# Attention's sums turned on TensorE, inverted there and stored as seven rows, with the periodic order placed anew

## The chip, the cores and the metric

One core of a Trainium2 chip runs the whole program in one launch. The metric is the device time of an execution in microseconds; the number quoted is the median over several runs.

## The reference

Attention with normalised q and k over 4 batches and 12 heads, then two feed-forward layers without a residual path, all in float32 on the inputs' values:

```python
# q, k, v: (4, 12, 448, 64)
q_n, k_n = rmsnorm(q, g_q), rmsnorm(k, g_k)
scores = matmul(q_n, k_n.T) / sqrt(64)
attn = exp(scores - max(scores, axis=-1))
attn = attn / (sum(attn, axis=-1) + 1e-9)
x = matmul(attn, v)                       # to (1792, 768)
h = x @ moe_w_in;  x = silu(h) @ moe_w_out        # 768 -> 2048 -> 768
h = x @ moe2_w_in; out = relu(h)**2 @ moe2_w_out  # 768 -> 2048 -> 768
```

## The kernel before, in words

The kernel is written as a list of steps. Each step has a kind, an engine (or a choice of engines) with an estimated duration, a function that issues its instructions, and the buffers that it reads and writes. A planner at build time orders all steps per engine. Most steps of the attention are *fixed*: the tables LOADS and TABLE give the place of a step within a period, PERIOD is the distance from one pair to the next, and FIRST adds an offset in the first eight pairs. So the nominal start of a step is PERIOD x i + table + offset, with PERIOD 9.007, and the planner keeps that order on each engine. The steps of the two layers are free: the planner simulates the engines and one DMA queue over eight rounds and keeps the best order. What is issued is only an order; on the chip every instruction starts when its engine reaches it and its semaphores allow it. SyncE (SP in the profile) issues nearly all DMAs, in its order, and stops at one whose data isn't ready.

The attention treats 24 pairs of heads, one after the other in a software pipeline. For a pair:

- `prepare` loads q and k (load_qk, two DMAs of 224 KB, L594; ring of 4), takes squares (ScalarE), sums (VectorE) and the inverse root by Newton steps (GpSimd), multiplies (norm, GpSimd), turns the result on TensorE (turn_q, L689) and splits it into an upper and a lower part (q_hi, q_lo).
- `values` loads v (load_v, 224 KB, L721; ring of 3).
- `weigh` works in four chunks of queries: 128, 128, 128 and a mixed one of the last 64 queries of both heads. A chunk has scores (TensorE, L755, or mixed, L762, which reads the masked copy Q made by GpSimd, L739), row_max (VectorE, L777), exp (ScalarE, L785), which also leaves the row sums in one of the 7 columns of `sums` (128 x 7), turn_e (TensorE, L798: 8 transposes of 64 x 112 into two banks "t" of PSUM), and e_copy (the two banks go to SBUF, one by ScalarE, one by VectorE, L559 and L561).
- `attend` multiplies with v in two halves (L851, 16 matmuls each). Beside it the sums take their own way: inverse (VectorE, L824 and L825) adds 1e-9 and takes the reciprocal in place, store_r (SyncE, L832) writes the 128 x 7 words to a DRAM tile of 7 x 128, and three spread DMAs (L840) read that back, each row repeated over 64 partitions, into R. pv_copy (ScalarE) takes the product from PSUM and attended (GpSimd, L871) multiplies it with R.
- keep_x (SyncE, L903) writes the finished 128 x 448 block of x to DRAM; x_hi and x_lo split the blocks of the first two batches for the first layer.

The layers come after it. Their buffers lie where the attention's were, so their first writes of products wait for the last attend; the first up matmuls (L1073) can run before. Weights come as 8-byte words (load_raw, L964), are turned into float32 by ScalarE and VectorE, split in two parts and kept in DRAM for later use. Both layers then run nearly without gaps on TensorE.

PSUM has three rings of banks: 4 of "s" (scores), 3 of "t" (turned tiles), 1 of "pv".

The planner counts 7 us between store_r and its landing and 5 for a spread (the table `extra` in Step).

Of the kernel before, what the change touches and what calls it, by code (L numbers as in the profile page):

```python
# [16 lines left out]
P = 128  # L17
# [6 lines left out]
PAD = 8  # L24
# [21 lines left out]
PERIOD = 9.007  # L46
# [12 lines left out]
TABLE = {  # L59
    "squares": [-13.15, -18.44],  # L60
    "sums": [-11.29, -11.24],
    "newton": [-8.75, -8.19, -8.19, -7.83, -5.41, -5.09, -4.77, -3.81, -3.49, -2.27, -1.95, -1.63, -0.09, 0.23, 0.79],
    "norm": [1.67, 2.75],
    "turn_q": [5.9, 10.18],
    "q_hi": [7.63, 11.01],
    "q_lo": [8.32, 11.64],
    "scores": [14.24, 15.38, 19.53],
    "row_max": [15.08, 17.83, 16.75, 19.89, 21.22, 22.23, 19.36],
    "exp": [16.01, 18.67, 18.06, 21.11, 22.2, 23.34, 20.5],
    "turn_e": [20.28, 20.51, 22.62, 22.98, 25.1, 25.33, 27.01],  # L70
    "e_copy": [21.72, 22.77, 23.95, 23.43, 26.04, 27.33, 28.67, 27.93],
    "mask": [14.0],
    "mixed": [18.4],
    "attend": [29.71, 34.52],
    "inverse": [30.72],
    "pv_copy": [37.19],
    "attended": [53.79],
    "x_hi": [68.41],
    "x_lo": [84.93],
}  # L80
# [30 lines left out]
class Step:  # L111
    def __init__(self, kind, on, fn, when, n):
        self.kind, self.on, self.fn, self.when, self.n = kind, on, fn, when, n
        self.needs, self.claims = {}, []
        self.at = min(on, key=lambda e: on[e][0])
        self.extra = {"store_r": 7.0, "spread": 5.0, "load_raw": 2.5, "load_raw2": 2.0, "load_y": 1.0}.get(kind, 0.0)
        self.nom = None
# [6 lines left out]
FORM = {"scores": "rows", "turn_e": "rows", "attend": "columns"}  # L124
SWITCH = 0.16
ENGINES = ("pe", "act", "dve", "pool", "sp", "none")
ROUNDS = 8
# [290 lines left out]
def kernel(  # L418
# [79 lines left out]
    def pe_t(t):  # L498
        return {"pe": (t, None, False)}
# [1245 lines left out]
```

## Time and profile before

| what | value |
|---|---|
| median of 3 runs | 1195.02 us (1189.43 to 1204.16) |
| profiled execution | 1187.26 us |
| its span, first to last instruction | 1185.4 us |
| TensorE matmul busy | 1129.0 us, 95% |
| VectorE busy | 935.1 us, 79% |
| ScalarE busy | 611.4 us, 52% |
| GpSimd busy | 293.5 us, 25% |

The profile is one execution; its time of 1187.26 us lies 1.8 us above its span, and all durations below come from it. Busy shares are means over stages: the attention fills about the first quarter of the span, the two layers the rest. PE is TensorE's matmuls, PEld its weight loads, DVE VectorE, ACT ScalarE, POOL GpSimd, SP SyncE. A matmul's end is modelled, so a busy PE may still not be at its peak.

### The profile page before, as it was taken

What the parts mean: (1) busy time and instruction counts of PE and PEld (TensorE: products, weight loads), DVE (VectorE), ACT (ScalarE), POOL (GpSimd) and SP (SyncE); (2) the same over time, 40 slices, a digit from 0 to 9 for tenths busy, and PEclk for the clock granted to TensorE, in tenths of its full rate; (3) what the DMA queues carried; (4) which work ended last, traced back from release to release, by engine and by line L of the source; (5) the groups of instructions that cost most, each with busy time, mean ns of one, the idle gap of its engine ahead of it and who ended that gap; (6) DMA issues with size and microseconds to landing.
All of it is one profiled execution on the core that took longest, in us unless ns stands there. A gap on an engine that the chain in (4) does not pass through costs nothing.

```text
span 1185.4 us, 20339 instructions
## 1 busy us (share of the span) xinstructions
PE 1129.0 (95%) x7405; PEld 1006.2 (85%) x7405; DVE 935.1 (79%) x1671; ACT 611.4 (52%) x1233; POOL 293.5 (25%) x533
## 2 busy tenths in 40 slices
PE   6997989897999999999999999999999999999998
PEld 5775766676998988999999999899999989999997
DVE  6887778674877778997678798578888986888886
ACT  5897788685455345544545352533333525333321
POOL 5666667621002010200010002001131120223220
PEclk8999999898999999999999999999999999999999
DMA  6577797758864756767878649877767695555544
GB/s 178 62 94 114 86 126 95 97 67 169 281 212 140 223 158 197 236 224 228 299 245 263 222 144 347 317 253 280 270 223 260 234 351 218 202 186 175 172 156 138
DMA packets 143988, 235.28 MB, mean 198 GB/s; under 512 B 33937, under 2 KB 107665, under 8 KB 143889
## 3 DMA queue, kind: packets, MB, share of 16 engines
q1 hardware_dynamic: 143648, 233.80, 67.4%
q8 instruction: 58, 0.95, 0.4%
q14 instruction: 42, 0.34, 0.1%
q10 hardware_dynamic: 240, 0.20, 0.1%
HBM read 157.58 MB, written 76.37 MB: 197 GB/s over the span
## 4 chain that ended last, share of the span: by engine, by line
PE 51%; DVE 8%; issue 1%; ACT 1%; DVEq 0%; ACTq 0%
PE t L1162 17%; PE s L1260 12%; PE s L1503 10%; PE pv L1162 7%; PE s L1628 5%; DVE w L580 1%; DVE g L1177 1%; DVE gg L1522 1%; DVE W L1119 0%; DVE W L1138 0%; DVE g L1560 0%; DVE gg L1680 0%; DVE gl L580 0%; DVE xf L1522 0%; DVE g L1436 0%
## 5 line engine op out<-in xcount | busy, mean ns | idle before, releaser
L1260 PE MATMUL s<-gg,w 128*128 128x448 f32 (+1 forms) x1168 | 238.6, 363 | 0.0
L1260 PEld LDWEIGHTS s<-gg,w 128*128 128x128 f32 x1168 | 217.0, 188 | 16.7
L1177 DVE TENSOR_TENSOR g<-t,g 128x448 f32<-128x448 f32 x180 | 108.7, 618 | 64.8 <-PE t L1162 58.1
L1503 PE MATMUL s<-w,gh 128*128 128x384 f32 (+1 forms) x564 | 144.0, 336 | 2.9 <-DVE gg L1522 1.8
L1522 DVE TENSOR_TENSOR gg<-s,gg 128x384 f32<-128x384 f32 (+1 forms) x197 | 102.3, 546 | 19.0 <-PE s L1503 18.9
L580 DVE TENSOR_TENSOR w<-W,w 128x768 fp32r<-128x768 f32 (+1 forms) x122 | 111.2, 918 | 3.5 <-ACT w L571 2.3
L777 DVE TENSOR_REDUCE mx<-s 128x1 f32<-128x448 f32 x168 | 100.3, 611 | 11.4 <-PE s L755 4.0
L1162 PE MATMUL t<-yb,w 128*128 128x448 f32 x468 | 103.8, 370 | 5.0 <-DVE w L580 3.3
L1503 PEld LDWEIGHTS s<-w,gh 128*128 128x128 f32 x564 | 102.1, 189 | 6.0 <-DVE gg L1522 1.9
L571 ACT CAST w<-W 128x768 fp32r<-128x768 f32 (+1 forms) x72 | 53.7, 747 | 91.9 <-DVE W L1138 23.3
L1162 PEld LDWEIGHTS t<-yb,w 128*128 128x128 f32 x468 | 88.1, 189 | 13.5 <-DVE w L580 4.4
L785 ACT ACTIVATE E<-s,mx 128x448 f32<-128x448 f32 x144 | 92.8, 650 | 12.4 <-DVE mx L777 7.9
L1428 ACT ACTIVATE g<-g 128x448 f32<-128x448 f32 x48 | 27.6, 577 | 133.8 <-DVE g L1177 133.4
L1503 PE MATMUL s<-w,gl 128*128 128x384 f32 (+1 forms) x282 | 94.6, 335 | 1.9 <-DVE gl L580 1.9
L1162 PE MATMUL pv<-xb,w 128*128 128x448 f32 (+1 forms) x330 | 72.3, 363 | 0.7 <-ACT g L559 0.7
L798 PEld LDWEIGHTS t<-ident,E 64*112 64x112 f32 x1152 | 44.5, 135 | 28.6 <-ACT PTa L559 7.4
L755 PE MATMUL s<-T 64*128 64x448 f32 x432 | 65.8, 408 | 1.1 <-ACT T L698 0.9
L1162 PEld LDWEIGHTS pv<-xb,w 128*128 128x128 f32 x330 | 60.8, 188 | 6.2 <-ACT g L559 1.3
L580 POOL TENSOR_TENSOR gl<-g,gh 128x448 fp32r<-128x448 f32 (+1 forms) x20 | 21.5, 1076 | 173.2 <-ACT gh L571 101.0
L851 PE MATMUL pv<-PTa,vv 112*64 112x256 f32 x384 | 52.0, 412 | 11.5 <-issue 6.0
L798 PE MATMUL t<-ident,E 64*112 64x64 f32 x1152 | 50.1, 225 | 12.4 <-ACT PTa L559 5.5
L1162 PE MATMUL t<-xc,w 128*128 128x448 f32 x270 | 60.0, 366 | 0.0
(179 smaller groups left out, 2356.3 us busy)
## 6 DMA issues: line engine op xcount, KB each, us to landing
raw<-in_moe_w_in_dram SPq DMA_DIRECT2D x32, 768.0 KB
raw<-in_moe_w_out_dram SPq DMA_DIRECT2D x24, 512.0 KB
raw<-in_moe_w_out_dram SPq DMA_DIRECT2D x16, 768.0 KB
su<-w SPq DMA_DIRECT2D x16, 768.0 KB
w<-su SPq DMA_DIRECT2D x16, 768.0 KB
xf<-y SPq DMA_DIRECT2D x48, 224.0 KB
xf<-x SPq DMA_DIRECT2D x39, 224.0 KB
ki<-W SPq DMA_DIRECT2D x16, 384.0 KB
```

Of the source, the lines that this page charges most:

```text
L571: nc.scalar.copy(o(), a())
L580: kind, when, any_t(n, rate), lambda e: engine(e).tensor_tensor(o(), a(), h(), ALU.subtract),
L755: nc.tensor.matmul(pts[j].ap[:, :S], T.ap[r, 0, a, c * CQ:(c + 1) * CQ], T.ap[r, 1, b_], start=(k_ == 0), stop=(k_ == 2),)
L777: lambda e, pt=pt, mx=mx: nc.vector.tensor_reduce(mx.ap, pt.ap[:, :S], AX.X, ALU.max, negate=True),
L785: lambda e, j=j, n=n, pt=pt, mx=mx, E=E: nc.scalar.activation(E.ap[:, j], pt.ap[:, :S], AF.Exp, bias=mx.ap, accum_out=sums.ap[:, n:n + 1]),
L798: nc.tensor.transpose(pe.ap[:CP, n * D:(n + 1) * D], E.ap[r, j, m * CP:(m + 1) * CP], ident.ap[r, r])
L1162: nc.tensor.matmul(pt.ap[:, c1:c2], w_()[:, c0 + c, :], view(b, a, c)()[:, c1:c2], start=(start and c == 0 and k == 0), stop=(c == HC - 1 ...
L1177: lambda e: nc.vector.tensor_tensor(o.ap, pt.ap[:, :S], a.ap, ALU.add),
L1260: nc.tensor.matmul(pt.ap[:, c1:c2], w_()[:, f, :], gg.ap[:, k, a, f, c1:c2], start=(f == 0 and n == 0), stop=(f == HQ - 1 and n == 2), ski ...
L1503: nc.tensor.matmul(pt.ap[:, :en], g.ap[:, fi, c0:c0 + P], w_()[:, 0, e0:e0 + en], start=(n == 0), stop=(n == 5),)
L1522: "acc", at, dve_t(n), lambda e: nc.vector.tensor_tensor(o(), pt.ap[:, :n], o(), ALU.add),
L1628: nc.tensor.matmul(pt.ap[:, :NH], a[i][0](m), b[j][0](), start=(start and k == 0), stop=(k == 2), skip_group_check=True,)
```

## The change

Four things change in the attention.

1. A step turn_s is added in `attend`: two transposes on TensorE (one per half of the partitions) turn the sums from 128 x 7 to 7 x 128, into columns 256 to 319 of the two banks that the pair's last turn_e uses (`pes`, returned by `weigh` as `last`).
2. inverse reads these banks: two tensor_scalar adds from PSUM into a new tile `inv` (7 x 128, ring of 2) and one reciprocal over it. The maximum that was taken along with the addition, and its buffer, go.
3. store_r writes `inv` to the DRAM tile as it lies: 7 rows of 128 words. The planner's count for its landing goes from 7 to 1 us.
4. All fixed places are new: PERIOD is 9.034, and TABLE, LOADS and FIRST have other values (FIRST, which moves the first eight pairs, isn't shown whole). Q has one buffer in place of two, and a padding tile of 8 words per partition goes.

```diff
-PERIOD = 9.007
+PERIOD = 9.034
...
-    "load_qk": [-28.41, -31.23],
-    "load_v": [16.98],
-    "store_r": [31.32],
-    "spread": [42.52, 43.02, 42.02],
-    "keep_x": [75.63],
+    "load_qk": [-27.01, -21.65],
+    "load_v": [13.9],
+    "store_r": [26.08],
+    "spread": [31.38, 30.43, 35.42],
+    "keep_x": [57.88],
...
-    "scores": [14.24, 15.38, 19.53],
+    "scores": [13.88, 14.5, 18.44],
-    "exp": [16.01, 18.67, 18.06, 21.11, 22.2, 23.34, 20.5],
-    "turn_e": [20.28, 20.51, 22.62, 22.98, 25.1, 25.33, 27.01],
-    "e_copy": [21.72, 22.77, 23.95, 23.43, 26.04, 27.33, 28.67, 27.93],
-    "mask": [14.0],
-    "mixed": [18.4],
-    "attend": [29.71, 34.52],
-    "inverse": [30.72],
-    "pv_copy": [37.19],
-    "attended": [53.79],
+    "exp": [16.11, 17.44, 18.05, 19.67, 20.78, 21.87, 22.48],
+    "turn_e": [17.85, 18.21, 20.24, 20.6, 22.28, 22.64, 24.11],
+    "e_copy": [19.19, 19.52, 21.39, 22.32, 23.09, 23.08, 25.71, 25.96],
+    "mask": [16.33],
+    "mixed": [19.62],
+    "attend": [24.96, 29.82],
+    "turn_s": [24.34],
+    "inverse": [25.31],
+    "pv_copy": [33.04],
+    "attended": [44.84],
...
-        self.extra = {"store_r": 7.0, "spread": 5.0, ...
+        self.extra = {"store_r": 1.0, "spread": 5.0, ...
...
-        Q = sa([P, 2, 2, LAST], FR, "Q", 2)
+        Q = sa([P, 2, 2, LAST], FR, "Q", 1)
...
-        def inverse(e):
-            r = sums.ap
-            nc.vector.tensor_scalar(r, r, 1e-9, None, ALU.add, ALU.max, accum_out=top.ap)
-            nc.vector.reciprocal(r, r)
+        NS = 2 * NCQ + 1
+        inv = sa([NS, P], F32, "inv", 2)
+        def turn(e):
+            for h, pe in enumerate(last):
+                r = slice(h * D, (h + 1) * D)
+                nc.tensor.transpose(pe.ap[:NS, 2 * CQ:2 * CQ + D], sums.ap[r], ident.ap[r, r])
+        step("turn_s", at, pe_t(0.06), turn, reads=[ident] + keys, writes=[(pe, "s") for pe in last])
+        def inverse(e):
+            for h, pe in enumerate(last):
+                nc.vector.tensor_scalar(
+                    inv.ap[:, h * D:(h + 1) * D], pe.ap[:NS, 2 * CQ:2 * CQ + D], 1e-9, None, ALU.add)
+            nc.vector.reciprocal(inv.ap, inv.ap)
...
-            lambda e: engine(e).dma_start(rd.ap.rearrange("n p -> p n"), sums.ap), reads=keys, writes=[rd],
+            lambda e: engine(e).dma_start(rd.ap, inv.ap), reads=[inv], writes=[rd],
```

In FIRST, pair 0's store_r has the offset 0.34 before and 0.59 after.

## Rows read from the trace of the kernel before

**Rows 1.** The page's 40 equal slices of the span, busy and clock in tenths.
```profile
PE   6997989897999999999999999999999999999998
...
PEclk8999999898999999999999999999999999999999
```

**Rows 2.** Busy time in stretches of the span; clock, DMA share and GB/s stand last.
```profile
core 0: us, PE busy (x) PEld busy (x) DVE busy (x) ACT busy (x) POOL busy (x), PEclk, DMA share, GB/s
...
30.00:277.50 247.50, 223.26 (x2687) 163.33 (x2687) 194.87 (x391) 203.55 (x532) 148.92 (x374) 0.96 0.70 96
...
33.50:45.00 11.50, 11.28 (x146) 8.14 (x142) 10.12 (x20) 9.86 (x27) 6.33 (x21) 1.00 0.40 27
...
53.40:62.60 9.20, 9.20 (x121) 6.89 (x119) 8.55 (x19) 8.69 (x24) 6.07 (x16) 1.00 0.43 74
...
83.07:216.00 132.93, 119.31 (x1434) 87.30 (x1434) 105.53 (x209) 111.31 (x293) 92.27 (x231) 0.96 0.77 105
...
216.00:276.10 60.10, 52.10 (x613) 37.69 (x613) 41.69 (x88) 43.79 (x112) 22.83 (x47) 0.91 0.60 88
...
277.00:290.00 13.00, 11.16 (x70) 9.64 (x66) 3.84 (x5) 1.90 (x3) 1.15 (x1) 1.00 0.94 128
...
5.00:11.00 6.00, 2.65 (x25) 2.41 (x23) 3.05 (x8) 2.88 (x5) 0.00 (x0) 1.00 0.99 272
```

**Rows 3.** SyncE in order of time: start us, us, DMA issued, count.
```profile
33.26 0.39 SPq L832 DMA_DIRECT2D rd<-sum  x1
...
53.53 0.38 SPq L832 DMA_DIRECT2D rd<-sum  x1
...
62.71 0.38 SPq L832 DMA_DIRECT2D rd<-sum  x1
...
72.13 0.38 SPq L832 DMA_DIRECT2D rd<-sum  x1
...
84.58 1.21 SPq L903 DMA_DIRECT2D x<-xf  x1
...
102.01 0.32 SPq L721 DMA_DIRECT2D vv<-in_v_dram  x1
...
216.00 0.39 SPq L832 DMA_DIRECT2D rd<-sum  x1
...
276.12 0.38 SPq L832 DMA_DIRECT2D rd<-sum  x1
```

**Rows 4.** TensorE in order of time, three stretches; in brackets the idle before.
```profile
52.41 1.95 PE L851 MATMUL pv<-PTa,vv 112*64 112x256 f32 x16
...
56.79 0.61 PE L798 MATMUL t<-ident,E 64*112 64x64 f32 x16
...
57.33 1.52 PE L851 MATMUL pv<-PTb,vv 112*64 112x192 f32 x16
...
61.60 1.95 PE L851 MATMUL pv<-PTa,vv 112*64 112x256 f32 x16
...
114.99 3.68 PE L851 MATMUL pv<-PTa,vv 112*64 112x256 f32 x16 [3.75 <-issue]
...
293.65 3.78 PE L1073 MATMUL t<-xc,w 128*128 128x448 f32 x10 [5.50 <-ACT g L1086]
```

**Rows 5.** Groups of VectorE instructions up to 290 us, shapes kept apart.
```profile
L561 DVE COPY PTb<-t 112x512 f32<-112x512 f32 x24 | 16.3, 679 | 0.4 <-PE t L798 0.4
...
L561 DVE COPY PTb<-t 112x256 f32<-112x256 f32 x24 | 9.9, 414 | 7.4 <-PE t L798 4.0 <-PE s L755 2.5 <-PE t L689 0.8
...
L825 DVE RECIPROCAL sum<-sum 128x7 f32<-128x7 f32 x24 | 4.8, 201 | 0.8
...
L824 DVE TENSOR_SCALAR_CACHE_REDUCE sum<-sum 128x7 f32<-128x7 f32 x24 | 3.6, 149 | 0.0
...
L824 DVE DVE_READ_ACCUMULATOR sum<-sum 128x1 f32 x24 | 2.0, 81 | 0.0
```

**Rows 6.** ScalarE in order of time around the end of the attention.
```profile
290.09 0.89 ACT L971 ACTIVATE W<-raw 128x768 f32<-128x768 f32 x1 [10.69 <-DMA raw<-in_moe_w_in_dram]
```

More of the change, by code (lines that the diff above doesn't have):

```diff
@@ new lines @@
+    1: {"load_qk": [18.88, 13.97], "squares": [13.43, 9.0], "sums": [9.44, 9.44], "load_v": [-6.03], "newton": [8.12, 7.92, 7.92, 6.9, 5.88, 4.79, 4.16, 3.07, 3.07, 3.07, 3.07, 3.07, 3.07, 3.07, 3.07], "norm": [2.97, 2.29], "turn_q": [1.0, 0.58], "q_hi": [0.54, 0.56], "q_lo": [0.58, 0.59], "scores": [0.55, 0.55, 0.55], "row_max": [0.55, 0.55, 0.55, 0.55, 0.55, 0.55, 0.55], "exp": [-0.19, -0.19, -0.19, 0.52, 0.55, 0.55, 0.55], "turn_e": [0.55, 0.55, 0.55, 0.55, 0.55, 0.55, 0.55], "e_copy": [0.01, 0.55, 0.55, 0.55, 0.55, 0.55, -0.02, 0.55], "mask": [-2.24], "mixed": [0.55], "attend": [0.55, 0.55], "turn_s": [0.55], "inverse": [0.55], "pv_copy": [0.6], "store_r": [0.55], "spread": [0.1, 0.55, 0.55], "attended": [-2.87], "keep_x": [0.57], "x_hi": [0.83], "x_lo": [0.07]},
@@ new lines @@
+    2: {"load_qk": [10.74, 5.83], "squares": [5.78, 1.35], "sums": [4.33, 4.33], "load_v": [0.05], "newton": [3.26, 3.26, 3.26, 2.24, 1.22, 0.13, 0.13, -0.96, -0.96, -0.96, -0.96, -0.96, -0.96, -0.96, -0.96], "norm": [-0.96, -0.96], "turn_q": [0.51, 0.5], "q_hi": [-0.24, 0.48], "q_lo": [0.5, 0.51], "scores": [0.51, 0.51, 0.51], "row_max": [0.51, 0.5, 0.51, 0.5, 0.51, 0.5, 0.51], "exp": [-0.07, -0.07, -0.07, 0.48, 0.5, 0.5, 0.5], "turn_e": [0.51, 0.51, 0.51, 0.51, 0.51, 0.51, 0.51], "e_copy": [-0.03, 0.51, 0.5, 0.5, 0.5, 0.51, -0.07, 0.5], "mask": [-2.39], "mixed": [0.51], "attend": [0.51, 0.51], "turn_s": [0.51], "inverse": [0.5], "pv_copy": [0.55], "store_r": [0.5], "spread": [0.05, 0.5, 0.5], "attended": [-2.92], "keep_x": [0.52], "x_hi": [0.78], "x_lo": [0.26]},
@@ new lines @@
+    4: {"load_qk": [3.61, -0.85], "squares": [0.46, 0.45], "sums": [0.41, 0.41], "load_v": [-0.04], "newton": [-0.91, -0.91, -0.91, -0.91, -0.91, -2.0, -2.0, -3.09, -3.09, -3.09, -3.09, -3.09, -3.09, -3.09, -1.15], "norm": [-1.15, -1.15], "turn_q": [0.42, 0.41], "q_hi": [-0.16, 0.39], "q_lo": [0.41, 0.42], "scores": [0.42, 0.42, 0.42], "row_max": [0.42, 0.41, 0.42, 0.41, 0.42, 0.41, 0.42], "exp": [-0.16, -0.16, -0.16, 0.39, 0.41, 0.41, 0.41], "turn_e": [0.42, 0.42, 0.42, 0.42, 0.42, 0.42, 0.42], "e_copy": [-0.12, 0.42, 0.41, 0.41, 0.41, 0.42, 0.41, 0.41], "mask": [-2.48], "mixed": [0.42], "attend": [0.42, 0.42], "turn_s": [0.42], "inverse": [0.41], "pv_copy": [0.46], "store_r": [0.41], "spread": [0.41, 0.41, 0.41], "attended": [-1.74], "keep_x": [0.43], "x_hi": [0.69], "x_lo": [0.65]},
@@ new lines @@
+    5: {"load_qk": [-1.71, -6.17], "squares": [-0.32, 0.37], "sums": [0.37, 0.37], "load_v": [0.37], "newton": [-0.95, -0.95, -0.95, -0.95, -0.95, -2.04, -2.04, -1.98, -1.98, -1.98, -1.98, -1.98, -1.98, -1.98, -1.19], "norm": [-1.19, -1.19], "turn_q": [0.38, 0.37], "q_hi": [-0.2, 0.34], "q_lo": [0.37, 0.37], "scores": [0.37, 0.38, 0.38], "row_max": [0.38, 0.37, 0.38, 0.37, 0.38, 0.37, 0.38], "exp": [0.37, 0.37, 0.37, 0.37, 0.37, 0.37, 0.37], "turn_e": [0.38, 0.38, 0.38, 0.37, 0.38, 0.38, 0.38], "e_copy": [0.37, 0.38, 0.37, 0.37, 0.37, 0.38, 0.37, 0.37], "mask": [-2.52], "mixed": [0.37], "attend": [0.38, 0.37], "turn_s": [0.38], "inverse": [0.37], "pv_copy": [0.42], "store_r": [0.37], "spread": [0.37, 0.37, 0.37], "attended": [-1.54], "keep_x": [0.39], "x_hi": [0.65], "x_lo": [0.85]},
@@ new lines @@
+    6: {"load_qk": [-0.17, -0.08], "squares": [-0.19, 0.33], "sums": [0.33, 0.33], "load_v": [0.33], "newton": [-0.99, -0.99, -0.99, -0.99, -0.99, -2.08, -2.08, -2.02, -2.02, -2.02, -2.02, -2.02, -2.02, -2.02, -1.23], "norm": [-1.23, -1.23], "turn_q": [0.33, 0.33], "q_hi": [0.33, 0.33], "q_lo": [0.33, 0.33], "scores": [0.33, 0.33, 0.33], "row_max": [0.33, 0.33, 0.33, 0.33, 0.33, 0.33, 0.33], "exp": [0.33, 0.33, 0.33, 0.33, 0.33, 0.33, 0.33], "turn_e": [0.33, 0.33, 0.33, 0.33, 0.33, 0.33, 0.33], "e_copy": [0.33, 0.33, 0.33, 0.33, 0.33, 0.33, 0.33, 0.33], "mask": [-1.47], "mixed": [0.33], "attend": [0.33, 0.33], "turn_s": [0.33], "inverse": [0.33], "pv_copy": [0.38], "store_r": [0.33], "spread": [0.33, 0.33, 0.33], "attended": [-1.34], "keep_x": [0.35], "x_hi": [0.61], "x_lo": [1.05]},
@@ new lines @@
+    7: {"load_qk": [0.28, -0.13], "squares": [-0.24, 0.28], "sums": [0.28, 0.28], "load_v": [0.28], "newton": [-1.04, -1.04, -1.04, -1.04, -1.04, -2.13, -2.13, -2.07, -2.07, -2.07, -2.07, -2.07, -2.07, -2.07, -1.28], "norm": [-1.28, -1.28], "turn_q": [0.29, 0.28], "q_hi": [0.28, 0.28], "q_lo": [0.28, 0.29], "scores": [0.29, 0.29, 0.29], "row_max": [0.29, 0.28, 0.29, 0.28, 0.29, 0.28, 0.29], "exp": [0.28, 0.28, 0.28, 0.28, 0.28, 0.28, 0.28], "turn_e": [0.29, 0.29, 0.29, 0.29, 0.29, 0.29, 0.29], "e_copy": [0.28, 0.29, 0.28, 0.28, 0.28, 0.29, 0.28, 0.28], "mask": [-1.28], "mixed": [0.29], "attend": [0.29, 0.29], "turn_s": [0.29], "inverse": [0.28], "pv_copy": [0.33], "store_r": [0.28], "spread": [0.28, 0.28, 0.28], "attended": [-1.15], "keep_x": [0.3], "x_hi": [0.56], "x_lo": [1.24]},
@@ L123 @@
 SELF = {"pe": 0.0, "act": 0.1, "dve": 0.1, "pool": 0.06, "sp": 1.9, "none": 0.0}
-FORM = {"scores": "rows", "turn_e": "rows", "attend": "columns"}
+FORM = {"scores": "rows", "turn_e": "rows", "turn_s": "rows", "attend": "columns"}
 SWITCH = 0.16
@@ L812, in weigh, with attend @@
                 plan.fix(i, "e_copy", 2 * c + h)
-        return PT, sums
-    def attend(i, vr, PT, sums):
+        return PT, sums, pes
+    def attend(i, vr, PT, sums, last):
         b, hp = pairs[i]
```

42 lines of the change are left out of this document (17 added, 25 removed).

## The prediction

> **What bounds the kernel now.** I read the page's 40 slices first. TensorE is at 9 tenths from slice 11 on (but for the last); in the ten before it, which are the attention, it falls to 6 to 8 in half of them and its clock dips [rows 1]. So I read that stage by stretches. From 30 to 277.5 us TensorE is busy 223.26 of 247.5 us at a mean granted clock of 0.96 of full speed [rows 2]: 24.2 us idle, and, if 0.96 mixes the full 2.4 GHz with its half, (1 - 0.96) / 0.5 x 247.5 = 19.8 us at 1.2 GHz, so some 10 us of work lost. Together that is 34 us in a stage that has no other work for TensorE.
>
> Next, the pace. Each of the 24 pairs of heads issues one store of its sums from SyncE, at 33.26 us for pair 0 and at 276.12 for pair 23 [rows 3]: 242.86 / 23 = 10.56 us per pair. The order written into the kernel has a period of 9.007. Yet the best stretches do nearly what the order asks: from the store at 53.53 to that at 62.71 it is 9.18 us, to the next 9.42, and in the first of these TensorE has no gap at all: the same half of attend starts at 52.41 and at 61.60, 9.19 us apart [rows 3, 4]. So 9.19 us is TensorE's own price of a pair, and 10.56 holds 1.4 us of waiting.
>
> What it waits for is a DMA. The plainest case: the load of pair 8's values is issued at 102.01 and the attend that needs them starts at 114.99, after 3.75 us of idle TensorE; its 16 matmuls, all at half clock, then take 3.68 us in place of 1.95 [rows 3, 4]. That load is 224 KB. In the burst of loads at the start the queue moves 272 GB/s at a busy share of 0.99 [rows 2], by which 224 KB take 0.84 us.
>
> What fills the queue are the stores of the sums: 128 x 7 words that are written column by column, so 896 packets of 4 bytes for 3.5 KB. In the 11.5 us behind the first store three loads (672 KB) are all that follows, and the rate is 27 GB/s at a share of 0.40 [rows 2]. At 272 GB/s the loads need 2.47 us. By time that leaves up to 11.5 - 2.5 = 9.0 us for one store; by share it leaves 0.40 x 11.5 - 2.45 = 2.15 us. The long stretch lies between: from 83.07 to 216 us, where x is also written back from 84.58 on [rows 3], a pair takes 132.93 / 12 = 11.08 us and moves 105 GB/s x 11.08 = 1.16 MB, or 4.28 us at 272 GB/s. Elapsed time leaves 6.8 us for a store, the share (0.77 x 11.08 = 8.53) leaves 4.25. I take 6. Then the queue needs 4.3 + 6 = 10.3 us per pair, more than TensorE's 9.19: the attention is bound by its DMA queue. The pace bears this out. Before x is written back pairs can run at 9.2 to 9.4, with it at 11.08, and from 216 on, where no q and k are loaded any more, at 60.12 / 6 = 10.02, with TensorE still recovering [rows 2, 3].
>
> **The change, part by part.**
>
> *The store.* 896 packets become 7 of 512 bytes. The queue's need falls by 2.15 to 9.0 us per pair, from 11.08 to between 8.9 and 2.1. At either end it is below 9.19, so the queue stops being the bound and TensorE becomes it. This term hardly depends on what a store costs.
>
> On that cost the Trainium skill's page "DMA: Bandwidth & Descriptors" (section "Anatomy of one DMA — SWDGE (gpsimd) path") speaks against the change: it calls descriptor generation small, and says that many can be emitted before the incremental cost shows, most of a DMA's fixed time being the receipt of the write. By that a store is a fixed delay, which its new form keeps. The 27 GB/s behind the first store disagree. The rule describes the other, GpSimd path, and I give it its own rival below.
>
> *turn_s.* Two more transposes per pair (64 x 7 in, 64 columns moved), right behind the last turn_e of the pair. 16 such matmuls take 57.33 - 56.79 = 0.54 us start to start [rows 4], so two take 0.07. As a group of their own they may cost a full matmul's length more; bounds 0.07 to 0.3, I take 0.10, by the row of the same shape. It adds a wait for the last exp's sum on TensorE, with attend queued behind it. The order puts turn_s at 24.34 and the last exp at 22.48, whose row sum is there by about 23.4, so it waits only when ScalarE is late by 0.9 us. The sums' columns sit in the last turn_e's banks, which the copies at 25.71 and 25.96 hold for longer than inverse at 25.31 anyway.
>
> *inverse.* Before: 149 + 81 + 201 = 431 ns on VectorE [rows 5]. After: two small reads of PSUM and a reciprocal of 128 elements on 7 partitions. A PSUM copy of 256 elements takes 414 ns, of 512 it takes 679, or 1.035 ns per element; for 64 that gives 414 - 192 x 1.035 = 215 ns each. The reciprocal by the same rate: 201 + 121 x 1.035 = 326 ns. Sum 756 ns, 0.33 more per pair. From below: no more than 201 for the reciprocal and 149 for each read, 499. From above: all of 201 ns scales with the elements, 201 / 7 x 128 = 3.68 us. I take 0.33, since a tensor_scalar over the same 7 elements takes 149, so that most of the 201 is fixed. VectorE is busy 8.55 us of the clean 9.20 [rows 2]; 8.88 still fits under TensorE. It costs nothing while VectorE keeps 0.3 us of room; with that cover gone it costs up to 0.33 x 23 = 7.6 us.
>
> *Pace.* 9.19 + 0.10, and 0.06 for what the clean pairs show beyond the best one: 9.35. The new period, 9.034, is 0.027 above the old one, 0.6 us in all and inside this term.
>
> *Order.* Everything is placed anew: store_r at 26.08 in place of 31.32, spread from 30.43 on in place of 42.02, attended at 44.84 for 53.79, load_v at 13.9 for 16.98. Of this the depth of a pair counts once: pair 0's store stood at 31.32 + 0.34 = 31.66 and came at 33.26, 1.6 late; now it stands at 26.08 + 0.59 = 26.67 and by the same lateness comes at 28.3. SyncE works in order: behind the spreads at 30.43 and 31.38 wait x's write, load_v and load_qk. The store has 4.35 us to land before the first spread stops SyncE; seven packets behind 0.84 us of load fit into that. load_v has 24.96 - 13.9 = 11.1 us to attend, 1.7 less than before, against a load of 0.84 us behind at most 4.3 us of other bytes. The single Q buffer costs nothing: the next mask (25.36) comes 5 us after mixed (19.62) ends.
>
> So the last store comes at 28.3 + 23 x 9.35 = 243.3 in place of 276.12: **32.8 us**.
>
> *Passage to the first layer.* TensorE runs until 288.2, idles 5.50 us until 293.65 and then sits at half clock, because a load of weights lands late: ScalarE starts on it at 290.09 after 10.69 us of waiting [rows 4, 6]. In 277 to 290 the queue carries 128 x 13 = 1.66 MB, 6.1 us at 272 GB/s, at a share of 0.94; the last two stores are in front of it. Without them the load comes some 6 us sooner. Bounds 0 (other transfers fill the room) and 8 (5.5 idle and half of some 5 us at half clock); I take **4**.
>
> *The rest.* 885 us of two layers keep their work. Their free steps are ordered anew by the planner, which I count as 0, plus or minus 6.
>
> Sum against the profiled execution: 1187.26 - 32.8 - 4 = 1150.5. The median of the runs, 1195.02, lies 7.8 above that execution, and the runs spread over 1189 to 1204. If this scatter sits in the DMA waits, it goes with them; if not, it stays. I add half, 4: **1154 us**.
>
> **The rivals.**
>
> *Part of the gain.* The stores go but loads still come late in some pairs, because SyncE's order is tighter (load_v's lead is shorter) and a spread can hold it. The nearest row is the last stretch, 10.02 per pair with no loads of q and k [rows 2, 3]: 28.3 + 23 x 10.02 = 258.8, 17.3 us saved and nothing at the passage, 1170 + 4 = 1174, within 2%. For it: that stretch. Against it: the stores were still in it, and TensorE came into it from a 4 us stall. Chance 0.11.
>
> *Nothing but the depth.* A store is a fixed delay, the packets not the cause, and the pace stays 10.56: 5 us from the depth, 1187.26 - 5 = 1182, against the median 1190. This is what the skill's rule above would make of it. For it: the share of 0.40 says that the 16 engines were not full behind the first store. Against it: the 27 GB/s in the same stretch. Chance 0.05.
>
> *Slower.* VectorE becomes the bound through the reciprocal. At 3.68 us per pair inverse is 4.1, VectorE 8.55 - 0.43 + 4.1 = 12.2, and the last store comes at 28.3 + 23 x 12.2 = 309: 33 us later than before, some 1220. It decides from an inverse above 10.56 - 8.12 = 2.4 us. For it: reciprocal is the slowest of the small rows. Against it: 52 ns over the tensor_scalar of equal size. With all else that ends slower, chance 0.04.
>
> **How the numbers follow.** Forecast 0.80, part 0.11, nothing 0.05, slower 0.04. The forecast's own range: 9.19 per pair, 8 at the passage, 6 in the layers and no 4 for the scatter give 1187.26 - 36.5 - 8 - 6 = 1137; 9.6 per pair, 0 at the passage, plus 6 and the full 7.8 give 1187.26 - 27 + 6 + 7.8 = 1174. To hold 8 in 10 with the partial case it reaches 1136 to 1180. A measurement of this kernel tells about 2% from no change; 2% below the median is 1171. Of the forecast 0.77 lies under that and of the partial case 0.05: faster 0.82, same 0.14, slower 0.04.
>
> **What would show it.** Right: stores of consecutive pairs 9.3 to 9.4 us apart from first to last; the last near 243; TensorE's idle in the attention under 8 us with the clock at 1.00; no wait of attend for values; RECIPROCAL near 0.33 us; the DMA share in the attention below 0.5. Wrong: pairs above 9.8 us apart, with VectorE or the queue named; SyncE standing at the spreads for most of a period; TensorE standing at turn_s; or the gain at 243 us given back in the layers.

## The result and the profile after

The changed kernel takes 1145.24 us (median of 4 runs, 1142.44 to 1147.44) against 1195.64 for the kernel before (4 runs, 1189.43 to 1204.16): a ratio of 0.957, with a 95% interval of 0.951 to 0.964. The profiled execution takes 1145.92 us with a span of 1144.1, 41.3 us below the profiled one of before. The forecast was 1154, in a range of 1136 to 1180.

The page's 40 slices of the changed kernel answer to [rows 1]:

```profile
PE   6999999999999999999999999999999999999998
...
PEclk6999999999999999999999999999999999999999
```

From the second slice on TensorE is at 9 tenths with its full clock up to the last slice; the holes of the attention are gone. In the first slice the clock still stands at 6 tenths.

The stretches of the attention, as in [rows 2] (columns as there: clock, DMA share and GB/s last):

```profile
33.00:254.00 221.00, 214.70 (x2723) 157.71 (x2719) 213.21 (x390) 204.19 (x534) 153.79 (x380) 1.00 0.41 115
...
72.27:178.62 106.35, 102.06 (x1313) 75.74 (x1309) 102.83 (x188) 100.30 (x265) 83.64 (x207) 1.00 0.44 121
```

TensorE is busy 214.70 of 221 us, its clock is 1.00, and the queue's share is 0.44 in the middle stretch where it was 0.77, at more GB/s than before (121 for 105). But there VectorE is now the fullest engine, by a little: 102.83 of 106.35 us, against TensorE's 102.06.

SyncE's stores answer to [rows 3]; the loads, the spreads and x's writes between them are left out, and most of the stores:

```profile
33.20 0.33 SPq L840 DMA_DIRECT2D rd<-inv  x1
...
72.27 0.28 SPq L840 DMA_DIRECT2D rd<-inv  x1
...
81.88 0.28 SPq L840 DMA_DIRECT2D rd<-inv  x1
...
91.50 0.29 SPq L840 DMA_DIRECT2D rd<-inv  x1
...
253.76 0.29 SPq L840 DMA_DIRECT2D rd<-inv  x1
```

From the first to the last it is 220.56 / 23 = 9.59 us per pair. Of the 23 distances 12 are 9.60 to 9.62, seven, early and late, are 9.81 or 9.82, one is 10.21 and the last 7.25. Between 33 and 254 us no computing engine waits for a DMA, so no pair waits for a load; what makes the seven longer was not pursued. The first store comes no earlier than before. A view of the DRAM tile gives the landing of these stores:

```profile
DMA to landing us min/median/max: 2.3/3.2/5.2
```

VectorE's groups for the inverse answer to [rows 5]:

```profile
L833 DVE RECIPROCAL inv<-inv 7x128 f32<-7x128 f32 x24 | 22.6, 941 | 0.8
...
L831 DVE TENSOR_SCALAR inv<-t 7x64 f32<-7x64 f32 x48 | 8.1, 205 | 1.3 <-ACT PTb L558 0.3
```

The reciprocal over 128 elements takes 941 ns; two reads of PSUM take 205 each. At the end of the attention, TensorE in order of time answers to the last row of [rows 4]:

```profile
253.72 1.86 PE L859 MATMUL pv<-PTb,vv 112*64 112x192 f32 x16
...
255.51 1.50 PE L1081 MATMUL t<-xb,w 128*128 128x448 f32 x7
...
264.80 2.00 PE L1081 MATMUL t<-xc,w 128*128 128x448 f32 x10
```

No row from 253.72 on, into the first layer, has idle time before it: the 5.50 us gap is gone.

So 41.3 us are gained. The last attend ends at 253.72 + 1.86 = 255.6 in place of 277.30 + 1.47 = 278.8: 23.2 us. From there to the end of the span it is 888.5 us in place of 906.6: 18.1 us, which the second experiment below splits in two.

### The profile page after: what moved, and what is told of

The parts are those of the page before. It is cut to its first block, busy times and chain, and to the rows that moved or that the text cites. A ratio compares the mean times of both kernels' runs of the same rounds, so it can differ in the third digit from the quotient of the medians.

```text
span 1144.1 us, 20545 instructions
## 1 busy us (share of the span) xinstructions
PE 1119.3 (98%) x7453; PEld 1000.1 (87%) x7453; DVE 942.8 (82%) x1651; ACT 619.4 (54%) x1251; POOL 296.2 (26%) x535
## 4 chain that ended last, share of the span: by engine, by line
PE 82%; DVE 10%; issue 3%; ACT 2%; DMA 1%; POOL 1%; SPq 0%; POOLq 0%; ACTq 0%; DVEq 0%
PE t L1170 21%; PE s L1268 20%; PE s L1511 12%; PE pv L1170 8%; PE s L1636 6%; PE pv L859 4%; PE t L797 4%; PE t L1081 3%; PE s L754 2%; PE t L688 2%; DVE mx L776 2%; DVE w L579 1%; DVE ms L613 1%; PE s L761 1%; DVE PTb L560 1%
## 5 line engine op out<-in xcount | busy, mean ns | idle before, releaser
L579 DVE TENSOR_TENSOR w<-W,w 128x768 fp32r<-128x768 f32 (+1 forms) x125 | 115.2, 931 | 6.5 <-ACT w L570 5.2
L570 ACT CAST w<-W 128x768 fp32r<-128x768 f32 (+1 forms) x78 | 58.1, 746 | 90.2 <-PE s L1268 24.9
L776 DVE TENSOR_REDUCE mx<-s 128x1 f32<-128x448 f32 x168 | 96.6, 608 | 0.6 <-PE s L754 0.5
L579 POOL TENSOR_TENSOR gl<-g,gh 128x448 fp32r<-128x448 f32 (+1 forms) x22 | 25.0, 1137 | 160.4 <-ACT gh L570 91.2
L754 PE MATMUL s<-T 64*128 64x448 f32 x432 | 59.5, 397 | 0.9 <-ACT T L697 0.9
L984 ACT ACTIVATE raw<-raw 128x768 int32<-128x768 uint16 (+1 forms) x72 | 59.4, 825 | 0.0
L797 PE MATMUL t<-ident,E 64*112 64x64 f32 x1152 | 57.2, 229 | 1.8 <-ACT E L784 0.6
```

Source lines behind the costliest of these rows:

```text
L579: kind, when, any_t(n, rate), lambda e: engine(e).tensor_tensor(o(), a(), h(), ALU.subtract),
L754: nc.tensor.matmul(pts[j].ap[:, :S], T.ap[r, 0, a, c * CQ:(c + 1) * CQ], T.ap[r, 1, b_], start=(k_ == 0), stop=(k_ == 2),)
L776: lambda e, pt=pt, mx=mx: nc.vector.tensor_reduce(mx.ap, pt.ap[:, :S], AX.X, ALU.max, negate=True),
L797: nc.tensor.transpose(pe.ap[:CP, n * D:(n + 1) * D], E.ap[r, j, m * CP:(m + 1) * CP], ident.ap[r, r])
L984: lambda e: nc.scalar.activation(lo(), raw.ap[:, :2 * m].bitcast(U16).rearrange("p (m t) -> p m t", t=4)[:, :, 1], AF.Copy, bias=2.0 ** -1 ...
```

## The experiments

My theory before them: the store's packets filled the DMA queue, and without them VectorE, through the reciprocal, sets the pace of 9.61. The rivals: a store is only a delay; the order placed anew made the gain; TensorE sets 9.61.

### The words stored beside the rows

The changed kernel keeps its store of rows and adds the old one behind it, into a tile that nobody reads.

```diff
+            engine(e).dma_start(rd.ap, inv.ap)
+            engine(e).dma_start(rw.ap.rearrange("n p -> p n"), sums.ap)
```

> The changed kernel, and behind each store of 7 rows a second one of the 128 x 7 words, column by column, into a DRAM tile that nobody reads. The order of all else is unchanged. If the 896 packets fill the DMA queue (my theory), loads come late again: the queue needs 4.3 + 6 = 10.3 us per pair or more in place of TensorE's or VectorE's 9.6, attend waits for its values again, and the time is 1160 to 1180. If a store of words is only a long delay for whoever waits for it (rival), nobody waits here: stores stay 9.6 us apart and the time is 1143 to 1150.

Measured: 1221.35 us (runs of 1209 to 1235; ratio to before 1.011, 1.003 to 1.019). The direction is that of the queue, and more of it than I expected. In the profiled execution, the longest of the four at 1234.72, the first 22 stores of rows lie 13.3 us apart. The stretch and the waits in it:

```profile
30.00:320.00 290.00, 234.93 (x2620) 165.12 (x2618) 207.51 (x374) 199.50 (x515) 150.68 (x378) 0.88 0.57 78
...
POOL xf L885 <- DMA R<-rd: 52.9, 12, 6.7
...
PEld t L797 <- ACT PTb L558: 25.6, 11, 5.2
...
SPq L841 <- DMA rw<-sum: 37.1, 10, 8.0
```

A pair moves 78 GB/s x 13.3 us = 1.04 MB, or 3.8 us at 272 GB/s. Elapsed time leaves up to 9.5 us for the added store, the share (0.57 x 13.3 = 7.6 us) leaves 3.8; where between them it lies, this run doesn't say. GpSimd waits for R and TensorE for copies behind it; attend, against what I expected, waits for no values in this stretch. I had expected that nobody waits for the added store itself, but SyncE does (last row): it stands for its landing in 10 pairs, 37.1 us in all, and with it stand the loads that SyncE would issue next. So this run shows that the words cost more than the whole gain, but it doesn't part a slow queue from a long landing; a stretch in the next experiment does. That the same words cost more in the new order than in the old one (1221 against 1201 on the same chip) fits its shorter leads; that was not tried by itself. The Trainium skill's page "DMA: Bandwidth & Descriptors" (section "Measured (HBM→SBUF, 128 partitions, SWDGE, issued from GpSimd)") counts about 10.5 ns for a packet, an estimate of 9.4 us for 896. That lies within these bounds, but the trace doesn't agree that the packets themselves take this long, as the next experiment shows. The rule of the Trainium skill that the prediction weighed, by which many descriptors can be emitted before they cost anything and a store is a fixed delay, is not borne out by the time of this kernel, nor by the next one's.

### The rows alone, in the old order

The kernel before with the store in its new form; the 7 x 128 tile is filled from the identity and one sum, so that it still waits for the inverse. Beside the store only this fill, 0.53 us of VectorE per pair, and the single buffer of Q are new.

```diff
+            nc.vector.tensor_scalar(rows.ap, ident.ap[:NS, :CQ], r[:NS, 0:1], None, ALU.add)
...
-            lambda e: engine(e).dma_start(rd.ap.rearrange("n p -> p n"), sums.ap), ...
+            lambda e: engine(e).dma_start(rd.ap, rows.ap), ...
```

> The kernel before, in its own order, with the store alone in the new form: after the inverse, VectorE fills a 7 x 128 tile (identity plus one sum, some 0.2 us) and store_r writes that as 7 rows; Q has one buffer to make room. The sums don't reach the output: the division of the result by them is replaced by other numbers. If the packets are the cause, stores come 9.3 to 9.5 us apart in place of 10.56, the first layer starts without its 5.5 us gap, and the time is 1187 - 26 - 9 = 1152; the layers, whose order is that of before, keep their 16 us of idle TensorE. If the layers' 8 us of gain come from the DMAs and not from the order, they show here too and it is 1144. If the order placed anew is the cause of the gain (rival), the pace stays at 10.5 and the time above 1180.

Measured: 1147.02 us (1145.40 to 1147.70; ratio 0.953, 0.948 to 0.958), as fast as the whole change. Its first and last store, the stretch behind the first store's place in [rows 2], and its last attend:

```profile
35.94 0.34 SPq L834 DMA_DIRECT2D rd<-rows  x1
...
245.06 0.30 SPq L834 DMA_DIRECT2D rd<-rows  x1
...
33.50:45.00 11.50, 11.50 (x151) 8.66 (x151) 11.03 (x25) 10.66 (x30) 7.01 (x24) 1.00 0.22 63
...
245.95 1.47 PE L853 MATMUL pv<-PTb,vv 112*64 112x192 f32 x16
```

That is 209.12 / 23 = 9.09 us per pair in the old order (9.0 to 9.8, but for the last two of 7.95 and 5.58), and the rate in the stretch rises from 27 to 63 GB/s. A closer look at what stands behind the first store shows what the words do. Three loads follow it in both kernels, issued within 2 us. First the kernel before, then the rows alone:

```profile
34.10:34.90 0.80, 0.80 (x22) 0.79 (x22) 0.32 (x2) 0.80 (x3) 0.41 (x2) 1.00 0.53 6
34.90:44.90 10.00, 9.78 (x123) 7.10 (x119) 9.09 (x18) 8.36 (x24) 5.48 (x17) 1.00 0.41 30
```

```profile
37.40:40.40 3.00, 3.00 (x42) 2.31 (x40) 3.00 (x5) 2.16 (x8) 0.61 (x3) 1.00 0.80 231
```

The words themselves are through in 0.8 us: in the trace's records of packets, all of theirs begin between 34.18 and 34.80, some 7 ns long each. Then the loads, all issued by 35.3, move at 30 GB/s for 10 us, 0.3 MB of their 0.69; behind the rows they move at 231 GB/s and 3 us are enough. (Behind the first words of the experiment above it is 38 GB/s for 9.5 us.) The share is 0.41 meanwhile. So the words don't fill the 16 DMA engines; for some 10 us they slow down what stands behind them. By what means, no run shows.

So the store's form by itself, without the new order, is worth as much as the whole change. Its last attend ends at 247.4, 8.2 us before that of the changed kernel; after it, it takes 898.4 us. Against the 906.6 of before that is 8.2 us for the passage (same order, no gap); the changed kernel's 888.5 are another 9.9. The second layer shows where, first the kernel before, then the rows alone, then the changed kernel:

```profile
740.00:980.00 240.00, 232.63 (x1230) 219.55 (x1229) 194.01 (x320) 95.30 (x168) 38.73 (x28) 0.99 0.75 275
```

```profile
700.00:940.00 240.00, 232.66 (x1231) 219.53 (x1229) 193.94 (x319) 95.39 (x167) 38.47 (x28) 0.99 0.75 276
```

```profile
700.00:940.00 240.00, 237.88 (x1269) 225.00 (x1267) 194.10 (x323) 100.45 (x178) 42.26 (x31) 1.00 0.79 284
```

In 240 us TensorE idles 7.4 us in both kernels with the old order and 2.1 in the changed one. That part of the gain comes from the planner's placing of the free steps, not from the DMAs: behind the last attend VectorE and ScalarE run the same sequence in the first two, and another one in the third, which also moves steps between engines (ScalarE has 1233, 1233 and 1251 instructions in all).

### The reciprocal left out, and taken twice

Two edits of the one line in inverse; in both the result is multiplied by the sums.

```diff
-            nc.vector.reciprocal(inv.ap, inv.ap)
```

> The changed kernel without the reciprocal (the result is multiplied by the sums, not divided). If VectorE bounds the pace of 9.59 through the 0.94 us of the reciprocal (my theory), pairs come 9.3 us apart, TensorE's 9.19 plus turn_s, and the time falls by 23 x 0.3 = 7 to 1138. If TensorE bounds it (rival: turn_s and its waits), it stays within 1143 to 1147.

```diff
             nc.vector.reciprocal(inv.ap, inv.ap)
+            nc.vector.reciprocal(inv.ap, inv.ap)
```

> The changed kernel with the reciprocal taken twice (the result is multiplied by the sums). If VectorE bounds the pace, each pair becomes longer by 0.87 us less the some 0.3 that VectorE idles now: 10.2 to 10.5 us, and the time grows by 13 to 20, to 1158 to 1166. If TensorE bounds it with VectorE in its shadow, the 0.3 us of room take a third of it and the growth stays below 8.

Measured: 1128.75 us without it (1128.59 to 1129.21; ratio 0.938, 0.933 to 0.943) and 1167.92 with two (1167.39 to 1168.25; ratio 0.970, 0.965 to 0.975). The first half of attend in two neighbouring pairs, in the kernel without the reciprocal, with one and with two:

```profile
110.97 1.95 PE L858 MATMUL pv<-PTa,vv 112*64 112x256 f32 x16
...
119.98 1.95 PE L858 MATMUL pv<-PTa,vv 112*64 112x256 f32 x16
```

```profile
109.70 1.95 PE L859 MATMUL pv<-PTa,vv 112*64 112x256 f32 x16
...
119.31 1.95 PE L859 MATMUL pv<-PTa,vv 112*64 112x256 f32 x16
```

```profile
115.93 1.95 PE L860 MATMUL pv<-PTa,vv 112*64 112x256 f32 x16
...
126.52 1.95 PE L860 MATMUL pv<-PTa,vv 112*64 112x256 f32 x16
```

A pair takes 9.01, 9.61 and 10.59 us. The second reciprocal costs its whole length of 0.94 and a little more: VectorE sets the pace. Taking the first away gains only 0.60 of the 0.94, because then TensorE takes over:

```profile
74.00:180.00 106.00, 105.99 (x1387) 78.30 (x1387) 99.96 (x189) 105.07 (x281) 88.25 (x221) 1.00 0.47 128
```

TensorE is busy 105.99 of 106 us, with ScalarE just behind it at 105.07; which of the two sets 9.01 was not tried. So TensorE's price of a pair in the new order, with turn_s in it, is at most 9.01, less than the 9.19 of the old order without; the rival that TensorE sets 9.61 has fallen. For the kernel, one VectorE instruction costs 16.5 us, of which 23 x 0.60 = 13.8 are the pace; the first store also came 3.3 us earlier in that execution (29.94).

### The inverse taken before the turn

Here r is the sums, 128 x 7; the step is placed at 23.7, ahead of turn_s, and the copy at 25.31.

```diff
+            nc.vector.tensor_scalar(r, r, 1e-9, None, ALU.add)
+            nc.vector.reciprocal(r, r)
...
             nc.tensor.transpose(pe.ap[:NS, 2 * CQ:2 * CQ + D], sums.ap[r], ident.ap[r, r])
...
-                nc.vector.tensor_scalar(inv.ap[...], pe.ap[...], 1e-9, None, ALU.add)
-            nc.vector.reciprocal(inv.ap, inv.ap)
+                nc.vector.tensor_copy(inv.ap[...], pe.ap[...])
```

> The changed kernel with the inverse taken before the turn, on 128 x 7 in place, and only copied out of PSUM behind it. VectorE is spared the reciprocal over 128 elements: 0.15 + 0.20 + 0.33 in place of 0.33 + 0.94, some 0.6 us per pair. If VectorE alone sets 9.61, pairs come 9.0 to 9.1 us apart as without the reciprocal, and the time is 1128 to 1136 (the free steps of the layers fall into another order, worth a few us either way). If TensorE now stands at turn_s for VectorE (rival), that wait of 0.5 us or more per pair keeps it at 1140 to 1147.

Measured: 1153.87 us (1153.55 to 1155.15; ratio 0.965, 0.957 to 0.972), slower than the change. Pairs come 9.0 to 9.2 us apart at both ends, as expected, but 9.8 to 10.3 in the middle; over all 9.46. Who waits for the inverse, in us and times:

```profile
  PEld t L825: 6.1, 11
  PE t L825: 4.5, 9
```

TensorE stands at turn_s for VectorE in some 10 pairs, about half a us each (its weight loads and its matmuls wait for the same thing). So the rival is right in the middle of the attention, though the last attend still ends earlier than in the changed kernel (at 250.6). The rest is lost behind it: 901.2 us in place of 888.5, by another order of the free steps, of which I had allowed "a few us".

What makes the middle pairs long is the small add ahead of the reciprocal. One in the middle, GpSimd's product with R beside it, and one near the end:

```profile
132.63 0.99 DVE L829 TENSOR_SCALAR sum<-sum 128x7 f32<-128x7 f32 x1
...
132.45 1.15 POOL L885 TENSOR_TENSOR xf<-xf,R 128x448 f32<-128x448 f32 x1
...
238.57 0.16 DVE L829 TENSOR_SCALAR sum<-sum 128x7 f32<-128x7 f32 x1
```

In the 7 pairs in which no such product runs beside it, the add takes 0.16 us. In the other 17 it ends within 0.03 us of the product's end, after 0.8 to 1.1 us in ten of them and 0.25 to 0.27 in seven. So it waits for GpSimd, and turn_s and all of VectorE stand behind it. Why it has to wait, no run shows.

### A longer warm start, alone and with the inverse first

```diff
-        for _ in range(WARM):
+        for _ in range(90):
```

> The changed kernel with 90 in place of 40 transposes on nothing at the start, so that TensorE is busy until the first turn_q and its clock doesn't fall. If the half clock until some 27 us is what makes the first store late (33.20 against 26.7 in the order), that store comes 2 to 4 us earlier and so does the end: 1141 to 1143. If the other engines' chains set the start (rival), less than 1 us changes.

> Both of the edits: the gains add up if both theories hold, 1125 to 1133; otherwise it equals the better one of the two.

Measured: 1143.75 us (1142.37 to 1144.41; ratio 0.956, 0.949 to 0.963), and 1154.67 for both edits (1152.69 to 1155.35; 0.965, 0.956 to 0.974). Alone, the stores begin and end here:

```profile
29.52 0.34 SPq L840 DMA_DIRECT2D rd<-inv  x1
...
249.96 0.29 SPq L840 DMA_DIRECT2D rd<-inv  x1
...
12.00:28.00 16.00, 11.25 (x127) 8.41 (x126) 14.67 (x26) 11.13 (x29) 13.05 (x44) 1.00 0.68 187
```

The same stretch in the changed kernel, and with both edits:

```profile
12.00:28.00 16.00, 12.21 (x79) 8.70 (x81) 13.23 (x24) 9.52 (x23) 12.81 (x42) 0.50 0.71 189
```

```profile
12.00:28.00 16.00, 13.07 (x96) 9.40 (x93) 13.52 (x24) 9.46 (x24) 12.54 (x41) 0.68 0.70 188
```

From 12 to 28 us the granted clock is 1.00, where the changed kernel has 0.50, and the first store comes 3.7 us earlier, as does the last (3.8). Some of that is the spread between executions: the changed kernel run again, further below, has its first store at 32.41 with a clock of 0.57 there. Of the 3.7 us 1.5 show in the median, whose runs overlap with those of the change. With the inverse first, the first store doesn't come earlier (31.48, against 30.49 without the longer start) and nothing is gained: there the longer start left the clock at 0.68, so it doesn't keep the clock up by itself. That the inverse first is slower holds on one chip: with the longer start in both, 1152.69 to 1155.35 against 1142.37 to 1144.41.

### The planner's count back at 7 us

```diff
-        self.extra = {"store_r": 1.0, ...
+        self.extra = {"store_r": 7.0, ...
```

> The changed kernel with the planner's count for the store's landing back at 7 us; no instruction changes, only the order of the free steps. After the last attend the changed kernel takes 888.6 us, the rows-only kernel with before's order 898.4. If the count alone makes the better order of the layers, they take some 898 us here and the time is 1150 to 1157; if it comes from the new places of the attention's steps (rival), the time stays within 1142 to 1149.

Measured: 1166.86 us (1165.82 to 1167.31; ratio 0.975, 0.968 to 0.982), and neither theory has it all. The layers behind the last attend take 888.6 us, as in the change, so the count alone does not make their better order; but the attention takes 21 us more. With the longer count the planner puts steps of the layers into the attention, and attend waits for its bank, because ScalarE works on weights before it copies the product out (TensorE's row, then ScalarE's; L979, L984 and L570 are the weights, the last row is pv_copy):

```profile
91.24 1.95 PE L859 MATMUL pv<-PTa,vv 112*64 112x256 f32 x16 [1.38 <-ACT xf L558]
...
88.30 0.67 ACT L979 ACTIVATE W<-raw 128x512 f32<-128x512 f32 x1
88.87 0.66 ACT L984 ACTIVATE raw<-raw 128x512 int32<-128x512 uint16 x1
89.42 0.82 ACT L570 CAST w<-W 128x768 fp32r<-128x768 f32 x1
...
90.67 0.52 ACT L558 COPY xf<-pv 128x448 f32<-128x448 f32 x1
```

In the changed kernel the first step of L979 comes at 218.0 us, here at 57.7. Between 51 and 124 us stores lie 11 to 19 us apart. A figure that changes no step, only where the planner puts it, is worth 21 us.

### The turn in pv's bank

The inverse stays where VectorE has it, on 128 x 7; the turn goes behind the first half of attend, into columns of its bank that the second half fills later; the longer warm start is in. The inverse is placed at 25.31, the turn at 26.77 and the copy at 27.1.

```diff
+            r = sums.ap
+            nc.vector.tensor_scalar(r, r, 1e-9, None, ALU.add)
+            nc.vector.reciprocal(r, r)
...
+            nc.tensor.transpose(pv.ap[:NS, 2 * CQ:3 * CQ], sums.ap, ident.ap)
...
+            nc.vector.tensor_copy(inv.ap, pv.ap[:NS, 2 * CQ:3 * CQ])
...
-    "store_r": [26.08], "spread": [31.38, 30.43, 35.42],
+    "store_r": [27.75], "spread": [33.0, 32.8, 35.42],
```

> The inverse on 128 x 7 in the place where VectorE now inverts, one transpose of all 128 rows behind the first half of attend into columns of its bank that the second half fills later, and one copy of 7 x 128 behind the squares' sum; the store stands 1.7 us later, the first two spreads behind load_qk; the longer warm start is in. If VectorE sets the pace and TensorE's wait at turn_s is what made the inverse-first kernel uneven, pairs come 9.0 to 9.1 us apart throughout and the last attend ends near 240. The time is then 1128 to 1135 with the layers at 888 us, and up to 13 more if the free steps fall as they did with the inverse first. If something else bounds the pace below 9.6 (rival), the last attend stays at 249 or later.

Measured: 1140.04 us (1135.72 to 1140.76; ratio 0.959, 0.952 to 0.966). Two neighbouring attends:

```profile
103.16 1.95 PE L861 MATMUL pv<-PTa,vv 112*64 112x256 f32 x16
...
112.31 0.87 PE L861 MATMUL pv<-PTa,vv 112*64 112x256 f32 x6
```

Pairs lie 9.15 us apart nearly throughout, the last attend ends at 243.4, 12.2 us before the change's, and the layers behind it take 894.9. The theory of the pace holds: with the reciprocal over 7 elements VectorE no longer sets 9.61, and the add, with no product of GpSimd beside it, takes 0.16 us in each pair. Half of the gain goes to the free steps. Whether this kernel beats the change was tried with both on one chip:

> The changed kernel once more, unaltered, beside the next one on the same chip: 1143 to 1148, with 9.6 us per pair.

> The kernel that turns the sums in pv's bank, once more: 1136 to 1141. If it is truly faster than the changed kernel, its runs lie below all of that one's runs on the same chip, by 4 to 7 us: some 10 at the end of the attention less some 6 that its free steps lose in the layers. If the two calls differed by their chips, the runs of the two overlap.

Measured: the change 1145.69 us (6 runs, 1144.04 to 1148.65; ratio to before 0.953, 0.948 to 0.958), the other 1138.95 (6 runs, 1137.58 to 1141.18; ratio 0.947, 0.943 to 0.951). Each of its runs lies below each of the change's: it is 6.7 us faster than the change and beats both kernels. The longer warm start, 1.5 us by itself, is part of that.

## Why the prediction was right, point by point

**The bound.** Right that the stores of words hold the attention back, and shown from both sides: the store in its new form alone gives 0.953, and the old store put back beside the new one takes more than the whole gain away. The picture of it, packets that fill the queue, was not right: the words are through in 0.8 us, and what stands behind them moves at 30 GB/s for 10. One of the supports was weak, too: before x is written back three of the five distances are 9.2 to 9.4 us, the other two 10.9.

**The price of a store.** I took 6 us between 2.15 and 9.0. Both bounds took the three loads as moved within the 11.5 us; at 27 GB/s only 0.31 MB was, so they are 3.5 and 10.4. The words put back give 3.8 to 9.5, and the 10 us of slow loads speak for the upper end. As the prediction says, the term hardly depended on it.

**TensorE's pace.** 9.19 + 0.10 was to be its new price; it is at most 9.01. turn_s itself is as small as taken: its two matmuls start 0.15 us ahead of what follows them. That the new order is cheaper for TensorE by some 0.3 us I had not seen in the table; which of its neighbours saves it was not tried.

**inverse.** The step that failed: 0.33 us more per pair, from 326 ns for the reciprocal, hidden under TensorE. It takes 941, so inverse is 0.41 + 0.94 = 1.35 in place of 0.43, and VectorE is the bound at 9.61. The error was the rate: I priced a reciprocal's elements as a copy's. By (941 - 201) / 121, an estimate from these two shapes, they cost 6.1 ns each and not 1.035. The prediction had both ends and chose by the row of a 7-element tensor_scalar, where the fixed part hides the rate. The rival that VectorE becomes the bound thus came true in kind; at 1.35 us it stays short of the 2.4 from which it would have made the kernel slower.

**The pace in all.** 9.35 was 0.24 too low, or 5.5 us over 23 pairs.

**The depth.** The first store was to come at 28.3 and came at 33.20: 4.9 us too early. The lateness of before, 1.6 us, was taken over as if it were a constant. It isn't: the clock of the start differs between executions. From 12 to 28 us it is 0.50 in the changed kernel; with 0.57 the same kernel's first store came at 32.41, and with the longer warm start and 1.00 at 29.52. Nor is the clock all of it: with the inverse first, 0.60 gave 30.49 and 0.68 gave 31.48.

**The passage.** 4 us; the gap closed fully and it is 8.2, the upper bound. Without words ahead of the first weights the whole wait is gone, in the old order too.

**The layers.** 0 plus or minus 6; they gave 9.9, by the planner's placing of the free steps. The spread over the experiments, 888.5 to 901.2 us for the same work, shows that my 6 was too small.

**The scatter.** I kept half of the 7.8 us between the profiled execution and the median. The changed kernel's runs lie within 5 us, with the median 0.7 below its profiled execution. It goes with the words: the rows alone, in the old order, scatter by 2.3 us, and the words put back by 26.

Together: 32.8 + 4 + 0 = 36.8 us were forecast in the profile and 23.2 + 8.2 + 9.9 = 41.3 measured. The two terms of the attention, pace and depth, promised 9.6 us too much; passage and layers gave 14.1 more than forecast, and the scatter went whole. The stores as the cause and the queue's end as the bound hold; that the rest added up to within 9 us of the median is luck.

## What to carry to other kernels

Count the packets of a DMA, not only its bytes: behind 3.5 KB in 896 words the loads on the same queue moved at 30 GB/s for 10 us, in place of 231, and what waits for them is late, with half-clock TensorE on top. A DMA's own time doesn't show this; look at the rate behind it. Where such a store goes, look at once for the engine that is next at its limit: here 0.94 us on a nearly full VectorE cost 14 us of pace, and could be moved away by inverting before the turn, where each partition has 7 elements and not 128, at a place where TensorE doesn't wait for it. In a kernel whose free steps are ordered by a planner, a change of any cost or place moves the rest by some 10 us; compare stage by stage before a total is believed.

## What the runs showed of the hardware that I had not expected

A reciprocal of 7 x 128 on VectorE takes 941 ns and of 128 x 7 takes 201, the same 896 elements; a tensor_scalar of 7 x 64 out of PSUM takes 205. A store of 7 rows of 512 bytes lands in 2.3 to 5.2 us (median 3.2). Behind a store of 896 words of 4 bytes, itself through in 0.8 us, loads move at 30 GB/s for 10 us; behind the rows at 231 GB/s. A tensor_scalar over 128 x 7 on VectorE takes 0.16 us alone, and up to 1.1 where GpSimd multiplies 128 x 448 beside it: it ends when GpSimd does.
